# Two transfer queues of a fused attention and state-space kernel in a new issue order

## The chip, the cores and the metric

The kernel runs on one core of a Trainium2 chip. That core has five instruction streams that run at the same time and meet only at semaphores: TensorE (PE in the profile; PEld is its loading of weights), VectorE (DVE), ScalarE (ACT), GpSimd (POOL) and SyncE (SP). SP computes nothing: it issues transfers. POOL here issues transfers and fills small pieces of memory with constants. The metric is device microseconds (us) of one execution, median of several; lower is better.

## The reference

Two independent layers on 2048 positions with 640 channels; their outputs are put side by side.

```python
# A: attention over 8 keys at distances 0, 2, ..., 14 (32 heads of 20 channels)
qkv = x @ wqkv
logits = einsum("bhsd,bhswd->bhsw", q, kg) * scale     # kg, vg: keys and values at s - 2w
o = einsum("bhsw,bhswd->bhsd", softmax(logits), vg)
a = o @ wo
# B: state-space convolution
K = einsum("dn,dnl,dn->dl", Cc, exp(dt * A * l), dt * Bc).real    # 2048 taps for each channel
y = irfft(rfft(u) * rfft(K))[:L] + u * Dskip                      # padded to 2L
out = concatenate([a, y], -1)
```

## The kernel before

**Part B** is done in five chunks of 128 channels, c = 0 to 4. The exponentials exp(dt·A·l) are built from tables. ScalarE writes the table of moduli, R, with many calls of Exp (`exps_chunk`, L256). Their argument is the tile LPB's part `alpha`, which holds dt times the real part of A, turned round by TensorE: `decays` (L163 and L166, copied out by L173) multiplies four blocks of 32 partitions of the tile B_A_re, u = 0 to 3, by a diagonal DG of dt. The phases come from B_A_im: VectorE splits them in three bfloat16 pieces hi, mid and lo (`fill`, L186 to L189, once for chunk 0 and once for chunks 1 to 4), transfers bring these to the tile LPA (L194) and LPB (L198), TensorE multiplies them by constants (L303, L307) and ScalarE takes the sine (L311, tiles TA and TX). VectorE multiplies R, TA, TX and the coefficients cT to forms (L332) and to Y (L366); TensorE contracts X with Y to the taps (`kgen_unit`, L380 and L385), and forward and backward transforms follow (L399, L407, L445), whose results Z go through the memory Zdram and Z4dram (L415) and come back in another layout (L773) to the last step of the transform (L787). The input u is in the tile U (L914, four transfers), the matrices of the transforms in BD, T2 and EA, the product of u and Dskip goes out as UDdram (L461) and comes back with Z.

**Part A** begins when part B has reached its last chunk: transposing loads of x (L500, tile xT), keys (L553), queries (L571), products of queries and keys (L601, L604), their sums over the channels (L615, tile ps_l, with the constant part of the tile wv), constants over the first rows of the logits ql (L621, on POOL: positions that a window does not have), a maximum over the windows (L624), the exponential (L639), the projection of the values (`proj_v`, L584: it needs the weights wv, which L532 loads), weights times values (L690, L697) and the output projection (L732) with the weights wo (L675). The outputs of the two layers leave by L739 and L791.

**The order of the work.** `body` writes the program in the order of its source; at its end `pin` gives each engine its own order: `ORDER` has for each of the five engines a string of runs, start+count in hexadecimal, numbers in that engine's source order. Each instruction gets a dependency on the one before it in the string.

```python
        order = [own[k] for start, count in runs for k in range(start, start + count)]
        for last, ins in zip(order, order[1:]):
            tc.add_manual_dep(ins, last.name, mybir.DependencyInfo(mybir.DependencyClass.NoSync, mybir.DependencyReason.DATA), reason="order")
```

So every queue runs through its string from left to right, and what an instruction waits for (the data, a free buffer, the transfer that used the same semaphore eight transfers ago) it waits for at its place. The four transfers of B_A_re are issued by ACT (u = 0 and 2) and SP (u = 1 and 3); in SP's string they are the numbers 3 (u = 1) and 4 (u = 3):

```python
            queue = {"B_A_re": (nc.scalar, nc.sync)[u % 2], "B_A_im": nc.gpsimd, "B_B_im": nc.gpsimd, "B_C_im": nc.gpsimd, "B_C_re": (nc.gpsimd, nc.sync)[u // 2]}.get(nm, nc.sync)
            queue.dma_start(out=nat[nm][32 * u:32 * u + 32], in_=src[u])
```

TensorE's string begins with `3+3 0+3 6+6`: its first three products are those of block u = 1, then come u = 0, 2 and 3. The load of wv is one transfer, and it may start when the logits of the first half are done:

```python
        behind(self.tc, self.nc.gpsimd.dma_start(out=self.wv, in_=self.wsrc[:, :, 2 * D:3 * D]), self.lact)
```

The first load of UDdram (`Inverse.load(0)`, L773, on POOL) writes a buffer that shares its place with tiles of the transforms. It waits for the last of their products and for the transfer Z4dram<-Z that reads the last Z.

Of the kernel before, what the change touches and what calls it, by code (L numbers as in the profile page):

```python
# [744 lines left out]
class Inverse:  # L745
# [107 lines left out]
    '1a8+1 1ad+1 1aa+1 1a5+1 1ae+1 1ac+1 1a6+1 1b1+1 1b3+1 1b0+1 1b2+1 1b4+1 1af+1 1b8+1 1b6+2 1ba+1 1b5+1 1bb+1 1bd+1 1b9+1 1be+2 1bc+1 1c0+2 1c3+1 1c2+1 '  # L853
    '1c6+2 1c5+1 1c4+1 1c8+2 1d0+1 1ca+1 1cd+1 1cb+1 1ce+2 1cc+1 1d1+1 1d3+2 1d2+1 1d6+2 1d5+1 1dc+1 1d8+3 1dd+2 1db+1 1e1+1 1e5+1 1df+2 1e6+1 1e2+3 1e8+2 '
    '1e7+1 1ea+1 1ed+1 1eb+1 1ee+3 1f2+1 1f1+1 1ec+1 1f4+1 1f3+1 1f5+3 1fe+1 1fd+1 1fc+1 1ff+2 1f9+1 1f8+1 203+1 1fa+2 204+1 201+2',
    '2+1 1+1 0+1 3+1 19+1 c+1 7+1 4+1 14+1 6+1 d+1 a+1 9+1 8+1 17+1 1a+1 b+1 e+2 5+1 11+1 10+1 15+1 13+1 12+1 1e+2 18+1 20+1 23+2 1b+2 22+1 21+1 1d+1 16+1 '
    '25+8 2e+1 2d+1 2f+5 36+1 34+2 37+3 3e+1 3a+1 3f+1 3b+1 40+2 3c+1 42+1 3d+1 43+5 4a+1 48+2 4c+1 51+1 50+1 4b+1 4d+3 52+1 54+1 53+1 56+1 55+1 59+1 58+1 '
    '57+1 5a+1 64+1 5b+1 62+1 5c+1 5e+1 61+1 60+1 63+1 6e+1 5d+1 68+1 5f+1 69+1 71+1 66+1 6b+1 65+1 6c+1 6a+1 72+1 67+1 70+1 6d+1 6f+1 76+1 75+1 7f+1 7c+1 '
    '7a+1 83+1 78+1 80+1 77+1 74+1 84+2 7e+1 81+1 7d+1 89+1 87+2 73+1 86+1 7b+1 8e+1 8a+1 79+1 82+1 8d+1 8b+1 90+1 8c+1 8f+1',
    '6+1 8+1 4+1 7+1 5+1 11+1 0+1 9+1 e+1 b+1 f+1 2e+1 10+1 2d+1 d+1 12+1 a+1 c+1 13+1 16+1 14+1 19+1 17+2 15+1 22+1 28+1 1c+1 1a+1 2a+1 1e+2 2b+1 26+1 '  # L860
    '20+1 23+1 27+1 21+1 25+1 3+1 1b+1 29+1 1d+1 2c+1 24+1 2f+1 33+1 30+1 2+1 31+2 1+1 35+3 3a+1 34+1 3b+3 39+1 38+1 3e+5 46+1 43+1 4a+1 49+1 45+1 47+2 '
    '44+1 4f+1 4b+2 4e+1 50+1 4d+1 51+2 54+1 53+1 55+3 5a+1 59+1 5b+1 58+1 5d+3 61+1 60+1 5c+1',
)


# [312 lines left out]
```

## Time and profile before

| | |
|---|---|
| median of 3 runs | 390.82 us (389.01 to 391.63) |
| span of the profiled execution, first to last instruction | 389.9 us |
| instructions in it | 18862 |
| transfers: packets, bytes | 39471, 43.30 MB |
| HBM read, written | 19.63 MB, 14.16 MB |

The profile gives no other time of that execution than its span; the median of the runs is 0.9 us over it. In lines of the timeline the first number is the start in us from the beginning of the span, the second the duration, then come engine, source line, operation and tiles (output<-input), and in square brackets how long the engine had been idle before, and what ended that. SPq stands for SP's issue of transfers, ACTq for ACT's. x42 means that 42 such instructions in a row are put together.

### The profile page before, as it was taken

The numbers are of one execution on the slowest core, as the hardware profiler recorded it, in microseconds if no ns is written. First come the engines' busy times: TensorE is split into PE (matmuls) and PEld (weight loads), VectorE is DVE, ScalarE is ACT, GpSimd is POOL, SyncE is SP. The second block draws the span as 40 slices with busy tenths as digits, with TensorE's granted clock in tenths as the row PEclk, the third lists the DMA queues.
The fourth block names the chain that finished last, engine by engine and source line by source line (L and its number), as shares of the span: only waits on it lengthen the run. The fifth ranks groups of instructions, "written<-read, shape, count | busy, mean of one in ns | idle before, by whom it ended". The sixth has DMA issues, their size and how long they took to land.

```text
span 389.9 us, 18862 instructions
## 1 busy us (share of the span) xinstructions
PE 338.0 (87%) x8677; PEld 250.9 (64%) x8677; DVE 356.1 (91%) x353; ACT 311.8 (80%) x524; POOL 49.9 (13%) x102
## 2 busy tenths in 40 slices
PE   1286989788898899988888999999999997789993
PEld 0275878677787778877777576556656775344561
DVE  8989899997999999999999998999988996897971
ACT  3999999799999999999998766455987746576761
POOL 8545001021000000100000100000030100011220
PEclk9998899699999999999999999999999999788998
DMA  6499304035021410151049662110773589399254
GB/s 161 109 192 208 121 13 163 6 103 121 29 84 34 109 32 31 57 131 40 2 118 152 144 133 71 34 30 2 166 248 100 163 192 204 70 254 282 81 141 110
DMA packets 39471, 43.30 MB, mean 111 GB/s; under 512 B 24768, under 2 KB 33952, under 8 KB 38752
## 3 DMA queue, kind: packets, MB, share of 16 engines
q1 hardware_dynamic: 34384, 29.34, 32.4%
q0 software_dynamic: 4112, 12.22, 11.5%
q8 instruction: 68, 1.11, 1.3%
q10 hardware_dynamic: 896, 0.54, 0.5%
q14 instruction: 11, 0.09, 0.1%
HBM read 19.63 MB, written 14.16 MB: 87 GB/s over the span
## 4 chain that ended last, share of the span: by engine, by line
PE 44%; ACT 25%; DVE 18%; issue 6%; DMA 4%; SPq 2%; POOL 0%; ACTq 0%; DVEq 0%; POOLq 0%
ACT R L256 7%; PE ps_k L553 6%; PE ps_q L571 6%; PE ps_v L584 6%; DVE Y L366 5%; ACT A L408 4%; DVE X L332 4%; PE ps_o L697 3%; ACT A L403 3%; PE ps_k L380 3%; PE ps_k L385 3%; PE ps_op L732 3%; PE ps_l L615 2%; PE ps_ia L445 2%; PE ps_f L399 2%
## 5 line engine op out<-in xcount | busy, mean ns | idle before, releaser
L366 DVE TENSOR_TENSOR Y<-PG 128x3072 bf16<-128x3072 bf16 x60 | 102.9, 1750 | 3.0 <-PE ps_k L385 2.8
L256 ACT ACTIVATE R<-LPB 128x192 bf16<-128x192 f32 (+1 forms) x169 | 57.7, 420 | 0.1
L380 PE MATMUL ps_k<-Y,X 128*32 128x64 bf16 x2176 | 46.9, 240 | 7.0 <-issue 2.7
L385 PE MATMUL ps_k<-Y,X 64*32 64x64 bf16 x2176 | 45.5, 234 | 0.7 <-issue 0.6
L380 PEld LDWEIGHTS <-X 128*32 128x32 bf16 x2176 | 34.8, 117 | 15.4 <-issue 6.8
L408 ACT CAST A<-ps_f 128x1024 bf16<-128x1024 f32 x40 | 40.4, 1038 | 3.5 <-PE ps_f L407 3.4
L385 PEld LDWEIGHTS <-X 64*32 64x32 bf16 x2176 | 32.8, 113 | 8.8 <-issue 1.1
L332 DVE TENSOR_TENSOR X<-R,TX 128x1536 bf16<-128x1536 bf16 x40 | 37.3, 950 | 0.3 <-PE ps_k L385 0.3
L311 ACT ACTIVATE TX<-ps_ph 128x768 bf16<-128x768 int16 x40 | 32.2, 838 | 3.7 <-PE ps_ph L307 3.7
L690 DVE TENSOR_TENSOR prod<-v,atp 128x1536 bf16<-128x1536 bf16 (+3 forms) x32 | 31.6, 1022 | 3.7 <-PE ps_o L697 3.7
L303 PE MATMUL ps_ph<-LPB,LPA 128*64 128x256 bf16 x288 | 29.3, 308 | 4.0 <-ACT A L408 1.3
L311 ACT ACTIVATE TA<-ps_ph 128x768 bf16<-128x768 int16 x30 | 24.3, 843 | 1.8 <-PE ps_ph L307 1.7
L407 PE MATMUL ps_f<-A,T 128*128 128x128 bf16 x320 | 22.3, 217 | 3.3 <-ACT A L408 1.3
L604 DVE TENSOR_TENSOR prod<-qT,kT 128x1024 bf16<-128x1024 bf16 (+1 forms) x16 | 22.9, 1486 | 1.2 <-ACT qT L572 0.8
L584 PE MATMUL ps_v<-xT,wv 128*32 128x512 bf16 x400 | 23.2, 379 | 0.0
L553 PE MATMUL ps_k<-xT,wkq 128*128 128x512 bf16 x100 | 23.1, 380 | 0.0
L407 PEld LDWEIGHTS <-T 128*128 128x128 bf16 x320 | 19.1, 96 | 6.1 <-issue 3.3
L571 PE MATMUL ps_q<-xT,wkq 128*128 128x512 bf16 x100 | 22.6, 379 | 0.0
L446 ACT CAST Z<-ps_ia 128x1024 bf16<-128x1024 f32 x20 | 19.6, 1014 | 3.4 <-PE ps_ia L445 2.2
L401 ACT ACTIVATE A<-ps_f,sign 128x1024 bf16<-128x1024 f32 x20 | 21.5, 1149 | 0.2 <-PE ps_f L399 0.2
L332 DVE TENSOR_TENSOR PG<-R,TA 128x768 bf16<-128x768 bf16 (+1 forms) x30 | 19.8, 685 | 1.8 <-ACT TA L311 1.3
L399 PE MATMUL ps_f<-BD,U 128*64 128x128 bf16 x320 | 21.0, 285 | 0.1
(157 smaller groups left out, 696.1 us busy)
## 6 DMA issues: line engine op xcount, KB each, us to landing
P<-A SPq DMA_DIRECT2D x16, 256.0 KB, 3.1
Zdram<-Z SPq DMA_DIRECT2D x16, 256.0 KB, 3.7
Z<-Zdram SPq DMA_DIRECT2D x8, 512.0 KB, 7.0
U<-in_B_u_dram SPq DMA_DIRECT2D x4, 640.0 KB, 9.5
UDdram<-UD POOLq DMA_DIRECT2D x10, 256.0 KB, 2.7
Z<-UDdram POOLq DMA_DIRECT2D x4, 640.0 KB, 6.7
out_dram<-ysb SPq DMA_DIRECT2D x32, 80.0 KB, 3.9
out_dram<-ob POOLq DMA_DIRECT2D x8, 160.0 KB, 3.4
```

Source lines behind the costliest of these rows:

```text
L256: exp = lambda o, i, m: nc.scalar.activation(out=o, in_=i, func=ACT.Exp, scale=m)
L311: last = nc.scalar.activation(out=dst, in_=words.rearrange("p b (q e f) -> p b q (e f)", e=8, f=4), func=ACT.Sin, scale=PI_LO / 32768.0)
L332: TT = lambda o, a, b, op: V.tensor_tensor(out=o, in0=a, in1=b, op=op)
L366: nc.vector.tensor_tensor(out=Y[:].rearrange("p q (b a) f -> p q b a f", a=8), in0=fa, in1=gb, op=A.mult)
L380: MM(ps[32 * g:32 * g + 32, t], lhsT=X[:, q, x, :, f], rhs=Ys[k][:, q, :, f], start=(t == 0 and n == 0), stop=False, tile_position=(0, 32 ...
L385: MM(ps[32 * g:32 * g + 32, t], lhsT=X[hb, q, x, :, f], rhs=Ys[k][hb, q, :, f], start=False, stop=(n == len(sets) - 1), tile_position=(64 ...
L407: last = MM(ps[:, kk], lhsT=C["T2"][:, 8 * b + kk, :], rhs=A1[:, :, 8 * b + kk, :], start=(kk % 4 == 0), stop=True, skip_group_check=True)
L408: nc.scalar.copy(out=A1[:, :, 8 * b:8 * b + 8, :], in_=ps[:].rearrange("p k (j g) -> p j k g", g=4))
L553: MM(ps[:, i], lhsT=self.wk[:, kt, 128 * ct:128 * ct + 128], rhs=self.x4[:, kt, 2 * i:2 * i + 2, 256 * hf:256 * hf + 256], start=(kt == 0) ...
L571: MM(ps[:, i], lhsT=self.wq[:, kt, 128 * ct:128 * ct + 128], rhs=self.x4[:, kt, 2 * i:2 * i + 2, 256 * hf:256 * hf + 256], start=(kt == 0) ...
L584: MM(ps[32 * sc:32 * sc + 32, i], lhsT=self.wv[:, kt, d + i::DH], rhs=self.xT[:, kt, 512 * sc:512 * sc + 512], start=(kt == 0), stop=(kt = ...
L690: nc.vector.tensor_tensor(out=p2.rearrange("p (d i) -> p d i", i=ni), in0=self.v2[:, 4 * j0:4 * j0 + 4 * nj, off:off + ni], in1=at[:, w, i ...
```

## The change

Two of the five strings of `ORDER` are new, those of SP and POOL. Nothing else differs: the strings of TensorE, VectorE and ScalarE are the same, and so are all instructions, tiles and buffers. In the diff's table two lines are shown, the beginning of SP's string.

```diff
@@ -853,13 +853,13 @@
-    '2+1 1+1 0+1 3+1 19+1 c+1 7+1 4+1 14+1 6+1 d+1 a+1 9+1 8+1 17+1 1a+1 b+1 e+2 5+1 11+1 10+1 15+1 13+1 12+1 1e+2 18+1 20+1 23+2 1b+2 22+1 21+1 1d+1 16+1 '
...
+    '0+3 7+2 c+1 9+2 5+2 d+1 b+1 f+1 1e+1 11+1 4+1 19+1 e+1 17+1 23+1 13+1 1a+1 14+1 12+1 16+1 10+1 1b+2 1f+1 18+1 3+1 24+1 1d+1 21+1 20+1 22+1 25+1 15+1 '
...
```

**Beginning of SP.** B_A_re are the real parts of A, Dn is Dskip, mix and ident are constants. Before, the third and the seventh row of SP's queue are the two loads of B_A_re, u = 1 first:

```order
L123 DMA ldt_105<-in_B_log_dt_dram 32x20 x2
L1140 DMA ident_58<-ident_c 128x128
L132 DMA B_A_re_112<-in_B_A_re_dram 32x5x192
L909 DMA Dn_223<-in_B_Dskip_dram 32x160
L132 DMA B_C_re_138<-in_B_C_re_dram 32x5x192
L140 DMA mix_124<-c_mix 128x288
L132 DMA B_A_re_112<-in_B_A_re_dram 32x5x192
```

After, twelve transfers of inputs and tables come first; then SP has these, the pieces of chunk 0 (names on 188 to 190), which wait for VectorE, with a quarter of U among them:

```order
L194 DMA LPA_101<-mid_189 32x2x192
L914 DMA U_84<-in_B_u_dram 32x64x160
L194 DMA LPA_101<-hi_188 32x2x192
L132 DMA B_A_re_112<-in_B_A_re_dram 32x5x192
L909 DMA Dn_223<-in_B_Dskip_dram 32x160
```

This B_A_re is block u = 3 (number 4). Block u = 1 (number 3) comes after the matrix T2 and behind two pieces of chunks 1 to 4 (hi_367 and mid_368), which wait for VectorE, and a third quarter of U:

```order
L194 DMA LPA_101<-mid_189 32x2x192
L907 DMA T2_76<-c_T2 128x4096
L194 DMA LPA_101<-lo_190 32x2x192
L194 DMA LPA_101<-hi_367 32x2x576
L194 DMA LPA_101<-mid_368 32x2x576
L914 DMA U_84<-in_B_u_dram 32x64x160
L909 DMA Dn_223<-in_B_Dskip_dram 32x160
L132 DMA B_A_re_112<-in_B_A_re_dram 32x5x192
L914 DMA U_84<-in_B_u_dram 32x64x160
```

What moved: the two loads of B_A_re, from the head of the queue to behind transfers that wait for VectorE, behind three quarters of U and behind T2.

**POOL at the middle of part A.** ql are the logits of the first half, wv and wo weights, HB a constant, Z_8512 and Z_9038 the first two quarters for the last transform. Before, POOL has:

```order
L621 MEMSET ql_7422 32x14
L621 MEMSET ql_7422 32x12
L621 MEMSET ql_7422 32x4
L621 MEMSET ql_7422 32x8
L621 MEMSET ql_7422 32x10
L532 DMA wv_7423<-in_A_wqkv_dram 128x5x640
L752 DMA HB_8510<-c_HB 96x2048
L675 DMA wo_8347<-in_A_wo_dram 32x5x640 x3
L773 DMA Z_8512<-UDdram_65 32x4x2560
L675 DMA wo_8347<-in_A_wo_dram 32x5x640
```

After:

```order
L675 DMA wo_8347<-in_A_wo_dram 32x5x640
L621 MEMSET ql_7422 32x6
L621 MEMSET ql_7422 32x2
L621 MEMSET ql_7422 32x4
L621 MEMSET ql_7422 32x12
L675 DMA wo_8347<-in_A_wo_dram 32x5x640
L621 MEMSET ql_7422 32x8
L621 MEMSET ql_7422 32x10
L675 DMA wo_8347<-in_A_wo_dram 32x5x640
L621 MEMSET ql_7422 32x14
L773 DMA Z_8512<-UDdram_65 32x4x2560
L532 DMA wv_7423<-in_A_wqkv_dram 128x5x640
```

What moved: the load of wv went from ahead of Z_8512's load to behind it, and three loads of wo went in among the constants of ql. HB and the last of the ten UDdram<-UD now stand ahead of the first wo, behind the load of the queries' weights.

**SP near the end.** Z_9360 is the last quarter for L787, ysb and ob are outputs of the layers. Before:

```order
L773 DMA Z_9360<-Zdram_63 32x4x2048
L791 DMA out_0_dram<-ysb_9037 32x2x640
L773 DMA Z_9360<-Z4dram_64 32x4x512
L791 DMA out_0_dram<-ysb_9037 32x2x640 x5
L773 DMA Z_9360<-Z4dram_64 32x4x512
L791 DMA out_0_dram<-ysb_9037 32x2x640
L773 DMA Z_9360<-Zdram_63 32x4x2048
L791 DMA out_0_dram<-ysb_9037 32x2x640 x6
```

After:

```order
L773 DMA Z_9360<-Z4dram_64 32x4x512
L791 DMA out_0_dram<-ysb_9037 32x2x640 x5
L773 DMA Z_9360<-Zdram_63 32x4x2048
L791 DMA out_0_dram<-ysb_9037 32x2x640 x3
L773 DMA Z_9360<-Zdram_63 32x4x2048
L791 DMA out_0_dram<-ysb_9037 32x2x640 x3
```

What moved: the last load of Z_9360 stood behind 13 of the 32 transfers out of ysb and stands behind 18. The other moves in the two strings are of the same kind: the order of writes to Zdram against the transposing loads of x and the loads of P, constants of R against UDdram<-UD, EA from ahead of U to behind the write of Sdram.

12 rows, old and new, of the table ORDER are left out of this document.

## The prediction

> **What bounds the kernel now.** I read the page first, then the chain of waits, then the busy time by stages, then the timeline at the places where the queues change. On the page VectorE is the busiest engine, but no engine is busy all the time:
>
> ```profile
> PE 338.0 (87%) x8677; PEld 250.9 (64%) x8677; DVE 356.1 (91%) x353; ACT 311.8 (80%) x524; POOL 49.9 (13%) x102
> ```
>
> The busy time by stages (start:end, length, then busy us of each engine, granted clock, share of the transfer engines, GB/s) says more:
>
> ```profile
> 8.56:29.10 20.54, 11.18 (x162) 9.55 (x162) 19.31 (x44) 19.74 (x62) 11.32 (x21) 1.00 0.87 154
> 29.10:100.00 70.90, 60.04 (x1910) 51.67 (x1910) 65.62 (x60) 67.87 (x120) 11.98 (x23) 0.90 0.41 105
> 100.00:210.00 110.00, 99.44 (x3193) 85.82 (x3188) 109.20 (x93) 108.86 (x182) 2.66 (x7) 1.00 0.24 61
> 210.00:302.60 92.60, 91.51 (x1821) 59.02 (x1825) 86.71 (x75) 62.11 (x73) 6.32 (x16) 1.00 0.46 109
> 302.60:328.30 25.70, 25.70 (x552) 18.10 (x545) 25.52 (x18) 16.92 (x21) 1.70 (x3) 1.00 0.77 187
> ```
>
> The reader is to see that each stage has an engine without a gap. From 8.56 to 29.10 it is ScalarE (19.74 of 20.54), to 210 ScalarE and VectorE together (108.86 and 109.20 of 110.00), to 302.60 TensorE (91.51 of 92.60), and to 328.30 TensorE with all of its 25.70. So a late start is not made up later: what stops the bound engine of a stage lengthens the run by nearly the same. Such are the two places where the new order makes a transfer late.
>
> **The first place: B_A_re.** In the timeline of before, the tables of part B begin so:
>
> ```profile
> 4.95 0.10 PEld L163 LDWEIGHTS <-B_A_re 32*128 32x128 bf16 x1 [4.95 <-DMA B_A_re<-in_B_A_re_dram]
> 5.95 0.18 PE L163 MATMUL ps_tr<-DG,B_A_re 32*128 32x32 bf16 x1 [5.95 <-DVE DG L156]
> 7.22 0.20 ACT L173 COPY LPB<-ps_tr 128x48 f32<-128x48 f32 x1 [0.32 <-PE ps_tr L166]
> 7.94 0.20 PE L163 MATMUL ps_tr<-DG,B_A_re 32*128 32x32 bf16 x1 [0.75 <-DMA B_A_re<-in_B_A_re_dram]
> 8.56 10.73 ACT L256 ACTIVATE R<-LPB 128x192 bf16<-128x192 f32 x42
> 26.58 1.51 ACT L311 ACTIVATE TX<-ps_ph 128x768 bf16<-128x768 int16 x2 [0.71 <-PE ps_ph L307]
> 29.12 0.96 DVE L332 TENSOR_TENSOR PG<-R,TA 128x1536 bf16<-128x1536 bf16 x1 [1.16 <-ACT TA L311]
> ```
>
> TensorE's first product is that of block u = 1. With that block missing TensorE does nothing, since its order is fixed; without the four blocks ScalarE has no argument for the 42 Exps at 8.56, and VectorE's first form at 29.12 waits for ScalarE's row behind them. Now block u = 1 stands in SP behind mid_368, a quarter of U and one Dn. When can it be issued?
>
> ```profile
> 12.58 0.26 DVE L188 CAST mid<-m 128x192 bf16<-128x192 f32 x1
> ...
> 23.70 0.56 DVE L188 CAST mid<-m 128x768 bf16<-128x768 f32 x1
> ...
> 17.82 2.11 SPq L914 DMA_DIRECT2D U<-in_B_u_dram  x2
> 19.97 3.32 SPq L909 DMA_DIRECT2D Dn<-in_B_Dskip_dram  x1
> ...
> 33.63 0.61 SPq L194 DMA_DIRECT2D LPA<-mid  x1
> ```
>
> mid_368 is there at 23.70 + 0.56 = 24.26, as before (what VectorE does up to there needs neither TensorE nor R). Then SP issues mid (0.61), U (half of 2.11, 1.05) and Dn (0.59, as long as another issue of 32 rows; the 3.32 shown is an issue held up behind two transfers of U), so B_A_re is issued at 26.5 at the earliest. Its landing, from the page and from the answers on transfers (KB, median us from issue to landing):
>
> ```profile
> B_A_re<-in_B_A_re_dram SPq DMA_DIRECT2D x2, 60.0 KB, 2.9
> Z<-Zdram SPq DMA_DIRECT2D x8, 512.0 KB, 7.0
> ...
> T<-c_T SPq DMA_DIRECT2D x1, 1024.0 KB, 5.2
> ...
> LPA<-hi SPq DMA_DIRECT2D x1, 72.0 KB, 9.7
> ...
> 19.00:29.00 10.00, 8.90 (x134) 7.55 (x130) 8.90 (x15) 9.20 (x22) 4.51 (x9) 1.00 1.23 185
> ```
>
> Lower bound: with an empty queue, 26.5 + 2.9 = 29.4. Upper bound: the LPA<-hi above is a small transfer behind two of U and took 9.7; with T2's 5.2 besides, 26.5 + 9.7 + 5.2 = 41.4. Between them I go by volume. mid_189, behind which U's first quarter stands, is ready at 12.58 + 0.26 = 12.84, so U starts at 13.5. From there three quarters of U, T2 and some 0.2 MB of pieces stand ahead of B_A_re in SP's queue: 3 × 0.66 + 1.05 + 0.2 = 3.2 MB. At the 185 GB/s of the last row, where U is moved, that is 17.3 us, to 30.8; with the 2.9 of its own row it lands at 33.7. T2 has long rows and moves at 1.05 MB in at most 5.2 us, over 200 GB/s; so I take 33.
>
> From the landing to the Exps: blocks 1, 0 and 2 took from 5.95 to 7.22 + 0.20 = 7.42, 1.47; the last block took 8.56 − 7.94 = 0.62, part of it beside the others; together about 1.9. The Exps start at 34.9 in place of 8.56, 26.3 later. ScalarE's gap of 0.71 at 26.58 will be gone, as everything it waits for is there: **25.6 us**, with bounds of 22.0 (landing at 29.4) and 34.0 (at 41.4). On ScalarE the rest has no gap to make it up.
>
> [...]
>
> **The second place: wv.** The chain around it, in the timelines of POOL, SP and TensorE, and the landings of single transfers:
>
> ```profile
> 286.93 0.86 POOL L532 DMA_DIRECT2D wv<-in_A_wqkv_dram  x1
> ...
> 288.32 1.72 POOL L675 DMA_DIRECT2D wo<-in_A_wo_dram  x3
> 308.68 0.56 POOL L773 DMA_DIRECT2D Z<-UDdram  x1 [18.64 <-PE ps_l L615]
> 309.23 0.59 POOL L675 DMA_DIRECT2D wo<-in_A_wo_dram  x1
> ...
> 304.08 0.33 SPq L415 DMA_DIRECT2D Z4dram<-Z  x1
> ...
> 302.02 0.73 PE L615 MATMUL ps_l<-prod,wv 128*32 128x256 bf16 x20
> 302.58 2.33 PE L584 MATMUL ps_v<-xT,wv 128*32 128x512 bf16 x40
> ...
> wv<-in_A_wqkv_dram POOLq DMA_DIRECT2D x1, 800.0 KB, 5.7
> ...
> wo<-in_A_wo_dram POOLq DMA_DIRECT2D x1, 200.0 KB, 10.3
> ...
> 309.40:318.80 9.40, 9.40 (x214) 6.68 (x210) 9.40 (x7) 4.61 (x6) 0.42 (x1) 1.00 1.00 232
> ```
>
> Before, wv has landed by 286.93 + 5.7 = 292.6, ten us ahead of its first use at 302.58. Now it stands behind Z<-UDdram, which waited at POOL until 308.68, for Z4dram<-Z (issued at 304.08) to land. wv takes the place that a wo has at 309.23. Lower bound of its landing: its own 5.7, so 314.9. The wo in that place took 10.3, to 319.5, because the transfer engines are full there (share 1.00, 232 GB/s). wv is 0.6 MB more than that wo, 2.6 us at 232 GB/s; so the upper bound is 318.8 + 2.6, rounded up to 322. I take 320, near the row of the same place. TensorE ends the sums before it at 302.75 and then stands until 320: **17.2 us**, bounds 12.2 and 19.3. In this stage TensorE has 25.70 of 25.70, so nothing makes it up; VectorE's products need TensorE's sums after two of them and stop too.
>
> [...]
>
> **The smaller parts.** wo among the constants of ql: VectorE's maximum waits for these.
>
> ```profile
> 285.85 0.43 DVE L624 TENSOR_TENSOR soft<-ql 128x512 bf16<-128x512 bf16 x1 [1.04 <-POOL ql L621]
> 286.86 0.89 DVE L624 TENSOR_TENSOR soft<-soft,ql 128x512 bf16<-128x512 bf16 x2 [0.59 <-POOL ql L621]
> ```
>
> Each wo takes POOL 0.59 to issue, so the constants come 0.6 to 0.7 later. Cover: TensorE works on the queries' projection meanwhile; without it the price is 0.7. I take 0. The first Zdram writes of chunk 3 now go ahead of the loads of P from Sdram: 0 to 1 under the same cover, taken as 0. Near the end the last load of Z_9360 goes behind five more outputs:
>
> ```profile
> 353.14 0.55 SPq L773 DMA_DIRECT2D Z<-Zdram  x1
> 353.73 3.85 SPq L791 DMA_DIRECT2D out_dram<-ysb  x5
> ...
> 364.10 0.59 PE L787 MATMUL ps_ib<-Z,HB 96*32 96x480 bf16 x12
> ```
>
> It is issued at about 357.6 and with the 7.0 of such a load, in the row above, it lands at 364.6, against a first use at 364.10: **0.5**, bounds 0 and 3.8 (if it lands as late as that wo, 10.3). The new places of T2, BD, EA, Dn, the constants of R, the transposing loads and UDdram's writes I cost at nothing: they are needed after 40, and at the start everything is now 25 us later than they are; each has 2 us or more of room. If one does not, it adds its own landing of 2 to 6.
>
> **Sum.** 25.6 + 17.2 + 0.5 = 43.3. Against the execution's own span, 389.9, that is 433.2; the median of the runs stands 0.9 over the span, so 434.1, and I say 434. All lower bounds together give 390.8 + 34.2 = 425, all upper ones 390.8 + 57.1 = 448.
>
> **Rivals.** First: transfers take only their own time, whatever is queued. Then both lower bounds hold, 425. For it speaks that SP's hold-ups (3.32) need two of U one after the other, and now other transfers lie between; against it the two rows of 9.7 and 10.3. [...]
>
> Second: only one of the two stalls shows, because TensorE or VectorE has room I don't see. Without the second it is 390.8 + 26.1 = 417. Against it stand the full rows of their stages.
>
> Third, on the other side: the queues do not hold back. If a transfer starts when its own data are ready, whatever waits ahead of it, B_A_re and wv land as early as before, and what is left is U's earlier start. The chain of waits has that on its path:
>
> ```profile
> 24.68 4.33 SPq L914
> 29.05 8.30 DMA LPA<-hi
> ```
>
> At most these 12.6 go, so 378; this decides if B_A_re lands before about 8. Against it speaks the wo at 309.23: it could have gone behind the three others, at 288.32 + 1.72 = 290.0, and went when the one ahead of it had gone. The same case covers that the new order is not carried out at all (390.8).
>
> **Chances.** The forecast, with both stalls about as priced, 0.78; the first rival 0.12; the second 0.06; the third 0.04. A measurement of this kernel can tell about 1% from no change. Of the third, 0.03 is for faster by over 1% and 0.01 for within 1%; all others are slower by over 1%, 0.96. The range leaves out the second and third rivals (0.10) and the far end of the upper bounds, which needs every transfer at its worst: 421 to 446.
>
> **What would show it.** In the changed profile: TensorE's first weights wait until 30 to 36 for B_A_re; the 42 Exps begin some 2 us later; VectorE's first form is near 55. L532 is issued right after the first Z<-UDdram, and L584 has a wait of 12 to 19 us for wv. Exps that begin before 20 would make the forecast wrong, and so would an L584 that does not wait.

## The result and the profile after

| | before | after |
|---|---|---|
| median, 4 runs each on one chip | 390.40 us (389.01 to 391.63) | 431.36 us (430.66 to 433.03) |
| span of the profiled execution | 389.9 us | 430.2 us |

The ratio is 1.1065 (95% interval 1.1026 to 1.1104): 41 us slower, 40.3 on the spans. The engines' busy time is nearly what it was (TensorE 335.3 us after 338.0); what grew is the span:

```profile
PE 335.3 (78%) x8677; PEld 249.6 (58%) x8677; DVE 355.7 (83%) x353; ACT 311.7 (72%) x524; POOL 49.0 (11%) x102
```

The stages of after, cut at the same instructions as in the prediction's table (columns as there), show where the new time lies:

```profile
8.56:36.90 28.34, 1.50 (x16) 1.23 (x16) 19.36 (x44) 0.70 (x4) 15.37 (x31) 1.00 1.02 198
36.90:57.45 20.55, 10.89 (x162) 9.32 (x161) 0.00 (x0) 19.73 (x62) 0.60 (x2) 1.00 0.13 30
...
238.30:329.00 90.70, 90.42 (x1751) 57.59 (x1747) 84.94 (x74) 61.21 (x71) 5.32 (x15) 1.00 0.42 104
329.00:347.58 18.58, 0.00 (x1) 0.00 (x1) 3.93 (x2) 2.98 (x4) 2.02 (x3) 0.62 0.80 215
347.58:374.80 27.22, 27.22 (x552) 18.37 (x561) 21.59 (x16) 13.87 (x17) 0.56 (x1) 0.95 0.30 64
374.80:430.20 55.40, 45.09 (x1056) 24.64 (x1056) 42.77 (x47) 34.24 (x63) 8.47 (x16) 0.99 0.68 175
```

Two rows are new: one of 28.34 us with ScalarE busy for 0.70, and one of 18.58 with TensorE busy for nothing. But the last row is shorter than before: from the end of the last L584 to the end of the span it was 389.88 - 328.34 = 61.5 us (its end is 323.85 + 4.49 in the timeline of before), and is 55.4.

**The first place.** The chain of waits of after (start, us, what):

```profile
24.52 0.58 SPq L194
...
25.15 0.59 SPq L914
...
25.79 3.28 SPq L909
...
29.12 5.93 DMA B_A_re<-in_B_A_re_dram
...
35.10 0.20 PE ps_tr L163
...
36.92 10.72 ACT R L256 x42
```

SP issues mid_368 when VectorE has made it, then a quarter of U, is held up for 3.28 us at Dn, and only then issues block u = 1, which lands at 35.05. VectorE's first form follows 20.5 us behind the first Exp, as before; ScalarE's gap ahead of it is still there (timeline):

```profile
54.93 1.51 ACT L311 ACTIVATE TX<-ps_ph 128x768 bf16<-128x768 int16 x2 [0.72 <-PE ps_ph L307]
...
57.47 0.96 DVE L332 TENSOR_TENSOR PG<-R,TA 128x1536 bf16<-128x1536 bf16 x1 [29.45 <-ACT TA L311]
```

**The second place.** POOL and TensorE in the timeline of after:

```profile
334.84 0.56 POOL L773 DMA_DIRECT2D Z<-UDdram  x1 [20.52 <-DMA Z4dram<-Z]
335.39 0.91 POOL L532 DMA_DIRECT2D wv<-in_A_wqkv_dram  x1
336.25 0.61 POOL L675 DMA_DIRECT2D wo<-in_A_wo_dram  x1
...
347.58 2.79 PE L584 MATMUL ps_v<-xT,wv 128*32 128x512 bf16 x24 [18.61 <-DMA wv<-in_A_wqkv_dram]
```

And the chain's piece between them:

```profile
335.39 12.15 DMA wv<-in_A_wqkv_dram
```

wv is issued right behind Z<-UDdram, takes 12.15 us beside the loads of Z, and TensorE stands for 18.61.

**The account.** The same instruction's start in both timelines gives the lag of after, stretch by stretch:

| instruction | before | after | lag |
|---|---|---|---|
| VectorE, first form (L332) | 29.12 | 57.47 | 28.35 |
| VectorE, L604 ahead of the wait for wv | 301.15 | 327.37 | 26.22 |
| VectorE, L656 behind it | 318.24 | 364.27 | 46.03 |
| TensorE, L732 | 352.33 | 392.47 | 40.14 |
| TensorE, L787 with the last load of Z | 364.10 | 405.90 | 41.80 |
| end of the span | 389.9 | 430.2 | 40.3 |

So 28.35 at the first place, 2.1 won back before the second, 19.8 at the second, 5.9 won back in the 30 us behind it, 1.7 lost at the last load of Z, and 1.5 won back to the end.

### The profile page after: what moved, and what is told of

Its sections match the earlier page's. It is cut to its first block, busy times and chain, and to the rows that moved or that the text cites. A ratio compares the mean times of both kernels' runs of the same rounds, so it can differ in the third digit from the quotient of the medians.

```text
span 430.2 us, 18859 instructions
## 1 busy us (share of the span) xinstructions
PE 335.3 (78%) x8677; PEld 249.6 (58%) x8677; DVE 355.7 (83%) x353; ACT 311.7 (72%) x524; POOL 49.0 (11%) x102
## 3 DMA queue, kind: packets, MB, share of 16 engines
q8 instruction: 68, 1.11, 1.1%
## 4 chain that ended last, share of the span: by engine, by line
PE 41%; DVE 22%; ACT 18%; DMA 10%; issue 6%; SPq 1%; POOL 1%; ACTq 0%; DVEq 0%; POOLq 0%
DVE Y L366 8%; ACT R L256 7%; PE ps_v L584 5%; PE ps_k L553 5%; PE ps_q L571 5%; DVE X L332 3%; DMA P<-A 3%; PE ps_o L697 3%; DMA wv<-in_A_wqkv_dram 3%; PE ps_k L380 3%; PE ps_k L385 3%; PE ps_x L732 3%; PE ps_op L732 2%; PE ps_ia L445 2%; PE ps_l L615 2%
## 5 line engine op out<-in xcount | busy, mean ns | idle before, releaser
L332 DVE TENSOR_TENSOR PG<-R,TA 128x768 bf16<-128x768 bf16 (+1 forms) x30 | 19.8, 685 | 30.2 <-ACT TA L311 29.6
L584 PE MATMUL ps_v<-xT,wv 128*32 128x512 bf16 x400 | 24.6, 396 | 18.6 <-DMA wv<-in_A_wqkv_dram 18.6
L604 DVE TENSOR_TENSOR prod<-qT,kT 128x1024 bf16<-128x1024 bf16 (+1 forms) x16 | 22.9, 1485 | 19.5 <-PE ps_l L615 19.4
L332 DVE TENSOR_TENSOR X<-R,TX 128x1536 bf16<-128x1536 bf16 x40 | 37.2, 949 | 0.1
L584 PEld LDWEIGHTS <-wv 128*32 128x32 bf16 x400 | 14.7, 140 | 25.8 <-DMA wv<-in_A_wqkv_dram 18.9
L163 PE MATMUL ps_tr<-DG,B_A_re 32*128 32x32 bf16 x20 | 1.9, 188 | 35.5 <-DMA B_A_re<-in_B_A_re_dram 35.1
L586 ACT CAST v<-ps_v 128x1024 bf16<-128x1024 f32 x10 | 10.0, 1012 | 24.8 <-PE ps_v L584 24.8
L173 ACT COPY LPB<-ps_tr 128x48 f32<-128x48 f32 (+1 forms) x8 | 2.1, 270 | 31.9 <-PE ps_tr L166 31.8
```

Of the source, the lines that this page charges most:

```text
L332: TT = lambda o, a, b, op: V.tensor_tensor(out=o, in0=a, in1=b, op=op)
L584: MM(ps[32 * sc:32 * sc + 32, i], lhsT=self.wv[:, kt, d + i::DH], rhs=self.xT[:, kt, 512 * sc:512 * sc + 512], start=(kt == 0), stop=(kt = ...
```

## The experiments

All change strings of SP and POOL alone, except the one with more traffic. In the strings 3 and 4 are the blocks u = 1 and u = 3 of B_A_re, 1e, 1f, 23 and 24 the quarters of U, 16 is T2; in POOL's, 44 is wv and 50 the first Z<-UDdram. Only the pieces that differ are shown. A ratio is to runs of the kernel before on the same chip, whose medians there were 389.5 (first four), 388.5 (second four) and 388.4 (last four).

### One place undone, and both

Block u = 1 back at the head of SP:

```diff
-'0+3 7+2 c+1
+'0+3 3+1 7+2 c+1
...
-18+1 3+1 24+1
+18+1 24+1
```

> The new order, but with SP's load of block u = 1 of B_A_re back at the head of SP. Theory: the late block costs what it is late, the 28.3 us by which VectorE's first form (57.47 against 29.12) came later, and nothing of it is made up; the 1.9 us that the new order has won back on VectorE between 84 and 115 belong to the new place of a write of UDdram, not to the late start, and stay. Then 431.4 - 28.3 = 403.1 us, with the Exps back near 8.6. Rival: the late start itself won the 1.9 back, since later transfers then lay clear of it; then they are lost again here: 405 us, and TensorE again has its wait of about 2 us at 70. By the forecast's 25.6: 405.8.

wv ahead of the load of Z:

```diff
-4a+1 50+1 44+1 4d+1
+4a+1 44+1 50+1 4d+1
```

> The new order, but with wv on POOL ahead of the first Z<-UDdram. Theory: the wait for wv costs 19.8 us at the place itself (VectorE's lag behind the kernel before rises there from 26.2 to 46.0), and gives back 5.8 us after it, because the loads of Z land while TensorE stands, so that TensorE's three waits of about 2 us at 330 to 350 (issue) get shorter. Without the wait both go: 431.4 - 19.8 + 5.8 = 417.4 us, with three waits of TensorE of 1.7 to 2 us after the last L584. Rival: the 5.8 come from the new order of the loads of Z, and stay: 411.6 us, with those waits as short as in the changed kernel. By the forecast (17.2, nothing given back): 414.

Both edits together:

> The new order with both undone: block u = 1 at the head of SP and wv ahead of the first Z<-UDdram. Theory: nothing is left but the 1.9 us of the write of UDdram on POOL: 390.4 - 1.9 = 388.5 us, give or take 1. Rival: the order of the loads of Z is worth the 5.8 us at the end: 383. Second rival: the other new places cost what the forecast left open (T2, BD, EA, the last load of Z): over 392.

| | us | ratio (95%) | first form |
|---|---|---|---|
| u = 1 first | 418.45 | 1.0772 (1.0674 to 1.0869) | 41.95 |
| wv first | 417.88 | 1.0767 (1.0693 to 1.0840) | 57.01 |
| both | 401.86 | 1.0367 (1.0269 to 1.0466) | 42.07 |

For wv the theory's 417.4 held; of its three waits of 1.7 to 2 us behind the last L584, two came, of 3.6 us in all. For u = 1 every expectation fell, the theory's and the rival's alike: 13 to 15 us too slow. For both together the theory's 388.5 fell by as much, and the second rival's "over 392" came true in the time but not by the transfers that it names: VectorE's first form is 12.95 us late with both undone. TensorE's timeline of that kernel says why:

```profile
20.89 0.20 PE L163 MATMUL ps_tr<-DG,B_A_re 32*128 32x32 bf16 x1 [13.26 <-DMA B_A_re<-in_B_A_re_dram]
...
29.27 1.07 PE L303 MATMUL ps_ph<-LPB,LPA 128*64 128x256 bf16 x8 [7.36 <-DMA LPA<-lo]
```

Block u = 3, the last of the four in TensorE's order, is late too: its load stands in SP behind mid_189 and a quarter of U. The longer stall had covered it. And behind that one waits another, for LPA<-lo.

### What made block u = 1 so late

U and T2 moved behind it, mid_368 still ahead:

```diff
-1e+1 11+1 4+1 19+1 e+1 17+1 23+1 13+1 1a+1 14+1 12+1 16+1 10+1 1b+2 1f+1 18+1 3+1 24+1
+11+1 4+1 19+1 e+1 17+1 13+1 1a+1 14+1 12+1 10+1 1b+2 3+1 1e+2 18+1 16+1 23+2
```

> The new order with SP's four loads of U and that of T2 moved behind the late block u = 1, which stays behind mid_368. It splits the lateness. Theory: SP waits at mid_368 up to 24.3 whatever else stands ahead, and the rest, from 24.3 to the landing at 35.0, is the large loads ahead (SP was held up 3.3 us behind them, and the landing took 5.9): without them it is issued at about 25 and lands in 2.9 at 28, the Exps start at 30 in place of 36.9, and the time is 424.5 us. Rival: the small pieces crowd the queue by themselves and the landing takes 5.9 again: issue at 25, landing at 31, 427.5 us. Second rival: the large loads do not matter: 431.

It took 424.61 us, ratio 1.0949 (1.0872 to 1.1025): the theory. Its chain:

```profile
24.36 0.58 SPq L194
...
24.99 2.25 DMA B_A_re<-in_B_A_re_dram
...
29.10 10.72 ACT R L256 x42
```

Without the large transfers ahead it is issued at 24.99 in place of 29.12 and lands in 2.25 in place of 5.93. These 7.8 us are those of U and T2 together; the other 20.5 of the 28.35 are the place in the order, behind a row that waits for VectorE (SP stood until 24.36 here as well, for mid_368).

### The stalls behind the stall

Both blocks at the head of SP, and wv first as above:

```diff
-'0+3 7+2 c+1
+'0+3 3+2 7+2 c+1
...
-11+1 4+1 19+1
+11+1 19+1
...
-18+1 3+1 24+1
+18+1 24+1
```

> The new order with blocks u = 1 and u = 3 of B_A_re both at the head of SP, and wv ahead of the first Z<-UDdram. Block u = 3 landed at 20.9 in the run with both undone, and the Exps waited for it until 21.5. Theory: a third late thing is hidden behind it: TensorE's first product of LPA stood there until 29.27 for LPA<-lo (17.55 before); ScalarE's first TA (21.58 before) then comes near 30.3, VectorE's first form near 37.5 and the time is 397 us. Rival: with the four blocks there nothing else is late: first form at 29 to 30, 388.5 us.

It took 400.96 us, 1.0319 (1.0263 to 1.0374), with the first form at 39.72. The theory's mechanism, but 4 us over its figure, 2.2 of them at the first form. Its chain:

```profile
22.06 0.58 SPq L907
22.69 6.03 DMA LPA<-lo
```

And TensorE's timeline:

```profile
28.86 1.07 PE L303 MATMUL ps_ph<-LPB,LPA 128*64 128x256 bf16 x8 [11.51 <-DMA LPA<-lo]
```

Then the pieces of chunk 0 together ahead of U and T2:

```diff
-f+1 1e+1 11+1 19+1 e+1 17+1 23+1 13+1 1a+1 14+1 12+1 16+1 10+1 1b+2
+f+1 11+1 e+1 13+1 12+1 10+1 1e+1 19+1 17+1 23+1 1a+1 14+1 16+1 1b+2
...
-17+1 1b+1 14+1 28+1
+17+1 14+1 1b+1 28+1
```

> The kernel of the last run, with the six pieces of LPA's first chunk on SP put together ahead of U, Dn, BD and T2, and POOL's last piece of that chunk ahead of the first piece of the next chunk. Theory: then nothing of the start is late, VectorE's first form is within 1 us of 29.1 and the time is 388.5 us, 1.7 below the kernel before through the write of UDdram. Rival: a fourth thing is late at the start (LPA or LPB of the next chunks, U, CN): first form beyond 31 and the time over 391.

392.18 us, 1.0096 (1.0061 to 1.0130); first form at 30.65, TensorE's wait for LPA<-lo down to 1.01. The start is 1.5 us late still, a little more than the theory allowed, and the time is nearer to the rival's. One more wait appears near the end, in TensorE's timeline:

```profile
323.71 0.39 PE L787 MATMUL ps_ib<-Z,HB 96*32 96x480 bf16 x4 [2.42 <-DMA Z<-Zdram]
```

So the end of both strings was put back as well, POOL's from the second Z<-UDdram on, SP's a little further up than the expectation says, from the loads of P from Sdram on. Of SP's string the first pieces:

```diff
-4c+2 51+1 4e+1 4b+1 50+1 4f+1 52+2
+4c+1 51+1 50+1 4b+1 4d+3 52+1
```

> The last kernel with everything of the start put right (first form 1.5 us late, 1% over the kernel before), with the order of SP from the write of Z4dram on, and of POOL from the second Z<-UDdram on, as before. Theory: what was left there was TensorE's waits for loads of Z (2.4 us at 323.7 and 1.6 at 364); they go, the time falls by 2 to 4 us to that of the kernel before (ratio 1.00, at most 1.005). Rival: the rest of the 1% is at the start; then the ratio stays at 1.01.

390.03 us, 1.0053 (1.0026 to 1.0079): between the theory and its rival. The 0.4% won over the kernel above is a comparison between two sets of runs and only likely. The two waits that the theory named are gone from its profile; in their place TensorE waits there for 4.1 us marked issue and 2.5 us for ScalarE's ysb. After all repairs a loss of 0.5% is left, of about the size of the 1.5 us by which the start is late; that it is the same loss is not shown.

### Does standing at L584 shorten the rest?

TensorE waits for nothing the profile can name ("issue") behind the last L584. From the summaries of waits over the 25 us behind it (line and what it waited for: us in total, times, longest), before, then after:

```profile
PE ps_o L697 <- issue: 5.7, 3, 2.0
```

```profile
PE ps_o L697 <- issue: 2.1, 2, 1.4
```

wv alone, moved in the kernel before:

```diff
-44+1 4f+1 4b+2 4e+1 50+1 4d+1
+4f+1 4b+2 4e+1 50+1 44+1 4d+1
```

> The kernel before with wv alone moved, on POOL behind the first Z<-UDdram; all loads of Z in the old order. Theory: TensorE stands some 18.6 us at L584 and 1.2 more go at a lower clock; the loads of Z land meanwhile, so that the stretch from the last L584 to the end is 55 to 56 us as in the three runs with wv late (55.4, 55.9, 55.9), in place of 58 to 61.5: 390 + 19.8 - 2 to 6 = 404 to 408 us. Rival: that stretch is short through the new order of the loads of Z; then it is 58 or more here, and the time 408 to 410.

406.16 us, 1.0496 (1.0437 to 1.0554). The time lies in the theory's range, but that range starts from 390; over this chip's 388.4 the loss is 17.0 to 21.5 us, which fits the rival's 18 to 20 better than the theory's 14 to 18. The stretch speaks for the theory: it is 55.1, in the profile of the shortest of the four executions (401.86; the others took 405.30 to 410.44). Its wait at L584 was 18.25, and behind it:

```profile
PE ps_o L697 <- issue: 1.6, 2, 1.3
```

How steady that is in the kernel before, two more profiles had to show:

> The kernel before, unchanged, for a second profile: how much do TensorE's waits marked issue differ from one execution to the next? If the wait of 2.16 us at 70.43 and the three of 1.7 to 2.0 us after the last L584 (5.7 in all; last L584 to the end 61.5 us) belong to the order of the work, they stand here again within 0.5 us. Rival: they depend on how a program's piece meets the transfers in that one execution; then some are missing or of other lengths here, the stretch after the last L584 differs by over 2 us, and the runs of one kernel differ by as much.

> The kernel before once more, for a third profile; what is expected is that of the second.

They gave 388.47 and 385.89 us. Neither side of the expectation held whole. The wait at 70 stands in the second profile and is missing in the third:

```profile
PE ps_k L380 <- issue: 1.9, 1, 1.9
```

| kernels | loads of Z | last L584 to end | issue waits behind it |
|---|---|---|---|
| before, three profiles | old order | 61.5, 58.2, 57.9 | 5.7, 4.5, 3.7 |
| before with one other change (the two kernels of the next part) | old order | 57.9, 58.0 | 4.8, 3.9 |
| all of the start right, end put back | old order | 61.1 | 4.1 |
| wv on time: wv first; both; blocks and wv first | new order | 62.5, 61.8, 63.0 | 3.6, 4.1, 5.1 |
| wv late: after; u = 1 first; U behind | new order | 55.4, 55.9, 55.9 | 2.1, 0.9, 2.0 |
| wv late alone | old order | 55.1 | 1.6 |

With wv late the stretch is 55 to 56 us in either order of the loads, and the new order with wv on time has 61.8 to 63.0. So it is the standing that shortens the stretch, and not the new order. In the old order the gain is 2 to 6 us, depending on which execution it is held against: four of the six profiles with wv on time have about 58, and the 61.5 is that of the longest of before's four executions. So some 3 us of what after won back there belong to that one execution of before. The kernel with the pieces together has 55.8 with wv on time: there TensorE's L584s took 30.05 us in place of 25.76, 2.42 of the difference in the wait at 323.71. That a short stand helps in the same way as a long one is not shown.

### Where the waits marked issue come from

The second write of UDdram ahead of constants of R, in the kernel before:

```diff
-2f+1 33+1 30+1 2+1 31+2
+2f+2 33+1 2+1 31+2
```

> The kernel before, with one change on POOL: the second write of UDdram (62.00) goes ahead of the constants of R (L249), for which POOL stood until 61.54. Theory: before, this write, the next one and that of Sdram crowd the transfer engines from 62 to 69, TensorE's next piece of program comes late behind them, and TensorE stands 2.16 us at 70.43 with nothing to wait for that the profile shows; with the write out of the way (near 53) that wait falls to under 0.6 and VectorE wins about 1.7 us by 115: 388.7 against 390.4. Rival: the 1.7 come from elsewhere in the new order: the wait at 70 stays and the time is the same.

The wait at 70 was gone in its profile, and the time the same: 388.79 us, 0.9992 (0.9959 to 1.0024). Since one of three profiles of before has no such wait either, this tells nothing of its cause, and the theory's 1.7 us are not there on the median.

Two more transfers beside TensorE's small products, in the kernel before; they are added work whose result nothing reads:

```diff
+    for k in range(2):
+        nc.sync.dma_start(out=pools["extra"][:, k], in_=Sd)
     pin(tc)
...
-2f+5 36+1
+2f+3 91+2 32+2 36+1
```

> The kernel before, with two more transfers of 1 MB, Sdram to a second DRAM buffer that nothing reads, on SP behind the third P<-A (issued near 137.6, where the transfer engines are idle, share 0.02 from 140 to 150). It tries the cause of TensorE's waits alone. Theory: TensorE's own program comes over the same transfer engines; full engines from 138 to about 147 make one or two pieces of it late, so that TensorE shows waits of 1.5 to 2.5 us marked issue in that window, where the kernel before has none over 0.6, and the time is 2 to 4 us longer. Rival: the waits come from the program itself (its many small products); then none appears there and the time is 390 to 391.

390.43 us, 1.0038 (1.0003 to 1.0073), or 0.1 to 2.8 us. The stretches with the added traffic (columns as in the stages):

```profile
138.00:140.00 2.00, 2.00 (x80) 1.62 (x78) 2.00 (x2) 2.00 (x3) 0.00 (x0) 1.00 1.01 332
140.00:142.00 2.00, 1.91 (x40) 1.60 (x37) 2.00 (x2) 2.00 (x4) 0.00 (x0) 1.00 1.04 393
142.00:144.00 2.00, 1.29 (x41) 0.95 (x40) 2.00 (x2) 2.00 (x4) 0.00 (x0) 1.00 0.98 356
```

And from the summary of TensorE's waits from 138 to 148:

```profile
PE ps_k L385 <- issue: 1.1, 1, 1.1
```

The same summary of before has no wait marked issue. With full transfer engines one of 1.1 appears, shorter than expected, and the time grew by about as much, less than the theory's 2 to 4 us. That supports the theory that TensorE's own program comes late behind transfers; one profile with one wait doesn't settle it.

The fourteen traces together say more. Each records the packets by which the program comes (the row q8 of a page: 68 packets of 16 KB). The traces have 40 waits of TensorE marked issue that are longer than 0.6 us. Two lie ahead of the first of these packets, at 22.7. The other 38 all end 1.2 to 1.8 us after such a packet has landed: the one that ends at 70.43 in before follows a packet that landed at 68.9. The 165 waits of that length that the profile puts down to something else end anywhere from 0.1 to 24 us after a packet. In the 3 us before the 38 packets start, the transfer engines have a median busy share of 1.03; before 872 other packets it is 0.28. So these waits end with the arrival of a piece of program, and mostly of one that came while the transfer engines were full. This is a coincidence in time, in every trace; it is not an experiment.

## Why the forecast was right, and which terms were off

The sign, both places and the sum were right: 434.1 against 431.36, 43.3 on the span against 40.3. The sum came nearer than its terms, in part by luck: the three terms were together 6.6 us too small, and 9.5 us were won back that the sum did not have.

| term | forecast (bounds) | measured |
|---|---|---|
| late B_A_re | 25.6 (22.0 to 34.0) | 28.35 |
| late wv | 17.2 (12.2 to 19.3) | 19.8 |
| last load of Z | 0.5 (0 to 3.8) | 1.7 |
| won back elsewhere | 0 | -2.1, -5.9 and -1.5 |

- **B_A_re, "issued at 26.5 at the earliest", landing at 33.** It was issued at 29.12 and landed at 35.05. The step that failed is Dn at 0.59: I took the hold-up of 3.32 behind two quarters of U for something that needs both in a row, and it came behind one, as 3.28. SP was in fact held up at the row behind each of the four quarters, for 1.61, 1.44, 3.28 and 3.31 us (at 14.26, 19.13, 25.79 and 30.45). The way from the landing to the Exps, 1.9, was right (35.05 to 36.92). The other 0.7 is ScalarE's gap, which I said would go. It did not: the row at 54.93 still shows 0.72. The bounds held, and going by volume gave a landing 2 us early.
- **"They are needed after 40, and at the start everything is now 25 us later than they are."** That cover was real, but it hid more than I listed. The first forms of the repaired kernels (42.07 and 39.72 against 29.12) show that block u = 3 would have cost 12.95 us by itself, and the pieces of LPA up to 10.6. I had named only u = 1. Putting it right alone is worth 13 us (431.36 to 418.45), not the 26 to 28 of the term.
- **wv, landing at 320 in the time of before.** The wait was 18.61 against 17.2, as wv took 12.15 from its issue. The other 1.2 is a cost I had not thought of, and it takes the term beyond its upper bound. Having stood, TensorE came back at half the clock, 0.50 (rows of after, granted clock third from the end):

```profile
331.00:334.80 3.80, 0.00 (x0) 0.00 (x0) 1.93 (x1) 0.99 (x2) 0.00 (x0) 0.82 0.67 276
334.80:338.20 3.40, 0.00 (x0) 0.00 (x0) 0.00 (x0) 0.00 (x0) 2.02 (x3) 0.50 0.79 167
...
347.60:349.30 1.70, 1.70 (x18) 0.70 (x21) 0.00 (x0) 0.00 (x0) 0.00 (x0) 0.50 0.13 30
349.30:351.00 1.70, 1.70 (x28) 0.84 (x24) 0.00 (x0) 0.00 (x0) 0.00 (x0) 0.65 0.00 0
351.00:352.70 1.70, 1.70 (x48) 1.30 (x44) 0.74 (x1) 1.01 (x1) 0.00 (x0) 1.00 0.00 0
```

The means place the drop near 333.4, 4.5 us after TensorE stopped at 328.97, and the return near 350.5, 2.9 us after it started again. So the L584s take 27.22 us in place of the 25.76 of before, 1.5 more. In the three other kernels with wv late the drop came 2.9 to 5.3 us after TensorE stopped, and the return 2.9 to 5.0 us after it started. The longest of their L584s took 0.643 to 0.646 us, as in after (0.645), against 0.438 in before.

- **"What stops the bound engine of a stage lengthens the run by nearly the same."** It held from 36.9 to 329, where 28.35 became 26.2; and of those 2.1 some 1.7 are TensorE's wait at 70 (2.16 in before, 0.47 in after), which not every execution of before has. It failed behind L584, by 5.9: in the last 60 us TensorE is not full (45.09 of 55.40 in after), its waits there depend on how far the transfers have got, and while it stood they got on. That is the likely reason, not one tried by itself, and waits are less than half of it. The same stretch of before has this row:

```profile
328.30:389.90 61.60, 48.86 (x1060) 25.80 (x1056) 42.92 (x47) 34.06 (x63) 8.50 (x16) 0.90 0.62 159
```

TensorE is busy for 48.86 us there, 3.8 more than in after for the same products. The granted clock of before is 0.50 from 336.0 to 342.8 and from 349.7 to 353.1, behind stands of TensorE of no more than 2.0 us each; after has no half clock between 350.5 and 429.0.
- **The last load of Z.** In place of the 7.0 taken, 9.0 passed from its issue to the landing, at 396.73 + 9.0 = 405.7. It is within the bounds. From the timeline:

```profile
396.73 0.55 SPq L773 DMA_DIRECT2D Z<-Zdram  x1
...
405.90 0.59 PE L787 MATMUL ps_ib<-Z,HB 96*32 96x480 bf16 x12 [1.89 <-ACT ob L706]
```

And from the summary of the loads of Z from 385 on:

```profile
DMA to landing us min/median/max: 2.8/6.0/9.0
```

The bracket names ScalarE's L706 as the releaser. But of the two L706 there the first ends at 404.95 and the second at 405.81, and in the run with wv first at 391.67 and 392.53, where L787 begins at 391.80: the first is too early here, the second too late there. The landing is 0.2 us ahead in both (405.70 and 391.60). It is the transfer.

**The rivals.** The first, own time alone, is out: wv took 12.15 (transfer engines at a share of 1.01 meanwhile) against 5.7 in before (0.85), B_A_re 5.93 against 2.25 without the large ones ahead. B_A_re, though only 60 KB, landed at 35.05, behind the quarter of U, 640 KB, that was issued 4 us ahead of it and took 8.2 (25.15 to 33.37). The second, only one stall shows, is out with 28.35 and 19.8 side by side, though its 417 is by accident what each single repair gives. The third is out with SP's and POOL's rows.

**What stays open.** Whether full transfer engines are all that makes the pieces of program late behind which the waits marked issue end; what the last 0.5% is. No order that was tried beats the kernel before.

## What to carry to other kernels

On a queue that issues in order, price a moved transfer by the row ahead of it that waits longest, and add the queue's large transfers: here they were 20.5 and 7.8 us. A late transfer can cover other late ones ahead of the same engine (here block u = 1 covered block u = 3, and that the pieces of LPA; with the one ahead repaired these held the first form back by 12.95 and by 10.6 us), so price each as if it were the only one; otherwise the repair of the first buys half of what the profile seems to promise (here 13 us of 28). Where an engine stands, look at what goes on meanwhile: here the clock that TensorE came back with, 0.50, cost 1.5 us behind the stall, and 5.9 us were won back there, likely through the transfers that had got ahead.

## What the runs showed of the hardware that was not expected

- SP was held up for 3.28 us at a transfer of 10 KB, Dn, behind a single quarter of U (25.79 in after), and for 6.23 us in the kernel with the pieces together. In the kernel with U behind block u = 1, Dn behind two quarters took 3.68, and the next two quarters 7.04 between them. Size alone is not what does it: in after the row behind T2, 1 MB against the 640 KB of a quarter, took 0.60 (23.00). T2 comes in rows of 4096 elements and U in rows of 160; whether that is the reason was not tried.
- After 18.6 us of standing TensorE ran at half clock (0.50 granted) for about 2.9 us, which cost about 1.5 us.
- The program comes over the transfer engines as well. The row below, from the page of after, has 68 packets in 1.11 MB, 16 KB each; TensorE has 17354 instructions in the profile (8677 products and as many loads of weights), which makes, as an estimate, 255 for each packet if all of them carry TensorE's program. In all, 38 waits of 0.6 to 3.0 us in fourteen traces end 1.2 to 1.8 us after such a packet; in before they are four, 7.8 of 389.9 us, and in after two, 2.1 of 430.2.

```profile
q8 instruction: 68, 1.11, 1.1%
```

- Executions of one kernel differ by such waits: the profiles of before have 3.7, 4.5 and 5.7 us of them behind L584, and 17 runs of it in one set lie between 386.1 and 390.4.
